# The product with the values in four 64x64 quarters of TensorE, its two key halves in two banks, and all eight PSUM banks given out by the planner

## The chip, the cores and the metric

The kernel runs on one core of one Trainium2 chip. The metric is the device time of one execution in microseconds (us). Before the change three runs gave a median of 1136.06 us (1135.74 to 1138.33).

TensorE (PE in the profile) multiplies into PSUM, which has eight banks of 512 float32 columns; VectorE (DVE) and ScalarE (ACT) copy results out of PSUM into SBUF; SyncE (SP) issues the transfers (DMA).

## The reference

Attention with "talking heads" for 4 batches, 12 heads, 448 tokens and heads of 64, followed by two MLPs over the 1792 tokens:

```python
scores = scale * np.matmul(q, k.transpose(0, 1, 3, 2))      # q, k, v: (4, 12, 448, 64)
scores = np.einsum('bhij,hg->bgij', scores, w_pre)          # heads mixed before the softmax
attn = np.exp(scores - np.max(scores, axis=-1, keepdims=True))
attn = attn / (np.sum(attn, axis=-1, keepdims=True) + 1e-09)
attn = np.einsum('bhij,hg->bgij', attn, w_post)             # heads mixed after it
x = np.matmul(attn, v)                                      # then (1792, 768)
h = x @ w_in;  x = (h * np.cos(h)) @ w_out                  # 768 -> 2048 -> 768
h = np.maximum(np.maximum(x @ w1, x @ w2), x @ w3)          # 768 -> 768, three times
out = h @ w_out2
```

The change touches only `np.matmul(attn, v)` and the places in PSUM of the steps around it.

## The kernel before

**Attention, the first 351 us.** A batch's 448 queries are cut into score blocks of 100 to 120 queries (4 blocks, 16 in all) and these into 10 "halves" (`HALVES`): one or two blocks whose mixed attention is kept together, 100, 120, 220 or 230 queries wide. For each block and head pair `qk` multiplies queries by keys (L566), `evac` copies the scores out, and `send` turns them by DMA into a grid in which 5 queries x 12 heads lie on the partitions. A block is then gone through in visits of up to 2 x 10 queries. A visit is `mix1` (L596, the first mixing of heads, into two banks), `rowmax` on DVE, `soft` (the exponential, on ACT), three small DVE steps up to `wscale`, `mix2` (L634, the second mixing of heads, which also turns keys onto the partitions, one bank for each of two slots), and `keep`, which copies `mix2`'s banks into the tile `a2` of the half. DVE and ACT share the copies `evac`, `keep` and `keepx` (all at L460).

**The product with the values** (`av`, L660 and L663) comes when a half is complete: three products for each half, one for two head pairs. The 448 keys lie as seven groups of 64, an odd number: three groups of pairs fill 128 partitions (L660, one instruction for 128 keys), and the seventh group lies half on the upper and half on the lower partitions, so that L663 multiplies half the queries at a time by 128 rows of which 64 hold zeros (the tile of `v` has two extra places, half of each zero). The four products of a column pass are two halves of 64 output partitions next to each other. The result of both head pairs goes to one bank; four or two `keepx` copies, each for a head pair and a block, then take it to the tiles `xs`, and `out` stores these to DRAM as the MLP's input `xT`.

**Banks.** Three rings are fixed: `ps_m` with 4 banks (`mix1`), `ps_t` with 2 (`mix2` and `av`), `ps_x` with 2 (scores; closed after the last scores, and then the first two banks of the MLP).

**What sets the order.** A planner (`Plan.run`) lists the steps with ranks, costs per engine and the rings that they take, and gives each engine, one after another, the step that can start soonest, the lower rank first among those that are close. Its order is the program order of every engine. For a step that may run on ACT or DVE it also chooses the engine. `behind` ties the three products of a half to visits of the next one, so that they are spread over those.

**The MLPs, from some 323 us to the end.** The first MLP's products (L160 to L162, three for each float32 product) fill in between the last visits and then go on without a break. ACT and DVE split inputs and weights into two parts for them (L147, L151 and others).

Of the kernel before, what the change touches and what calls it, by code (L numbers as in the profile page):

```python
# [33 lines left out]
BUFS = {"k": 12, "q": 18, "s": 8, "e": 6, "w2s": 3, "v": 7, "xs": 6, "a2": 2, "ps_m": 4, "ps_t": 2, "ps_x": 2}  # L34

RANK = {"fwget": 3.598, "fw": 2.0, "fwgap": 2.0, "fx": 3.474, "fxgap": 0.827, "x1": 2.568, "fh": 7.0, "fhgap": 0.483, "fa": 12.527}
WAIT = 0.034
KC = DM // 128
# [333 lines left out]
class Plan:  # L372
# [17 lines left out]
    def run(self, places):  # L390
# [6 lines left out]
        order = {key: n for n, key in enumerate(self.ops)}  # L397
        open_ = {key for key, n in waiting.items() if not n}
        while open_:
            best = {}  # L400
            for key in open_:
                rank, run, engines, after, takes, _ = self.ops[key]
                t = max([done[x] for x in after], default=-50.0)
                for n, ring in enumerate(takes):
                    back = places[ring] - takes[:n].count(ring)
# [18 lines left out]
            rank, run, engines, after, takes, _ = self.ops[key]  # L424
            for n, ring in enumerate(takes):
                taken[ring].append((key, takes[:n].count(ring)))
# [17 lines left out]
def attention(ctx, tc, q, k, v, w_pre, w_post, same_row, xT, tp, mlps):  # L444
# [9 lines left out]
    ps_m, ps_t = (psum(n, BUFS[n]) for n in ("ps_m", "ps_t"))  # L454
    ps_x = scores_only.enter_context(
        tc.tile_pool(name="ps_x", bufs=BUFS["ps_x"], side="right", space=bass.MemoryType.PSUM))
# [19 lines left out]
    begun = ps_m.tile([128, S], F32, name="mps")  # L476
# [76 lines left out]
    def score_bank(n, hp):  # L553
        grid = lambda: ps_t.tile([128, 512], F32, name="aps")[:, :S]
        return (("ps", lambda: ps_x.tile([128, S], F32, name="ps")), ("ps_t", grid),
                ("ps_m", lambda: ps_m.tile([128, S], F32, name="mps")))[hp % 3 if n == 0 else 0]

    def qk(n, hp, _):
        b, _, m = score[n][:3]
        x, i0 = half_of(n)  # L560
        for g in range(2):
            live["s", n, 2 * hp + g] = score_bank(n, hp)[1]()
# [6 lines left out]
    def stir(hp, x, _):  # L569
        if hp == x == 0:  # L570
            live["stir"] = ps_m.tile([128, S], F32, name="mps")
# [17 lines left out]
    def mix1(v, _):  # L589
        n, t, slots = visits[v]  # L590
        for a in range(2):
            live["m", v, a] = ps_m.tile([128, S], F32, name="mps")
# [34 lines left out]
    def mix2(v, _):  # L627
        slots = visits[v][2]
        for y in slots:
            live["a", v, y] = ps_t.tile([128, 512], F32, name="aps")[:, :JB * PH].rearrange("p (u m) -> p u m", m=PH)  # L630
# [15 lines left out]
    def pairs(x):  # L646
        return 2 * x, 2 * x + 1

    def av(half, x, _):
        b, _, _, m, _ = halves[half]  # L650
        a2, w = live["a2", half], m // 2
        both = ps_t.tile([128, 512], F32, name="aps")
        for n, hp in enumerate(pairs(x)):
            ps = live["av", hp] = both[:, n * NHALF:n * NHALF + m].rearrange("p (a w) -> p a w", a=2)
            for j in (*range(1, JP + 1), 0, JP + 1):
                for g in range(2):
                    of = live["v", b, hp][:, j, g, :]
                    to, rows = ps[64 * g:64 * g + 64], a2[:, :, 2 * hp + g, :w]
                    if 0 < j <= JP:
                        nc.tensor.matmul(to, of, rows[:, 2 * j - 2:2 * j], start=j == 1, stop=False)  # L660
                    else:
                        a = 0 if j else 1
                        nc.tensor.matmul(to[:, a], of, rows[:, 2 * JP], start=False, stop=j > 0)  # L663

    def keepx(half, hp, eng):

        xs = live["xs", hp] = xp.tile([128, NHALF], F32, name="xs")
        ps = live["av", hp]
# [33 lines left out]
    for n in range(NS):  # L702
        b = score[n][0]
        start, end = score[n - 1][0] != b or not n, n == NS - 1 or score[n + 1][0] != b
        for hp in range(HP):
            r = (first[n - 1] - 2.5 + 0.1 * score[n - 1][3] * hp) if n else -40.0 + hp
# [8 lines left out]
            ring = score_bank(n, hp)[0]  # L715
# [536 lines left out]
```

## Time and profile before

| | |
|---|---|
| median of 3 runs | 1136.06 us |
| profiled execution, its own time | 1134.89 us |
| its span, first to last instruction | 1133.1 us |
| last product with the values ends | 351 us |
| PE busy | 1112.5 us, 98% |
| DVE busy | 919.3 us, 81% |
| ACT busy | 663.0 us, 59% |

The page gives busy time by engine and in 40 slices of the span, the chain of work that ended last, and groups of instructions by line. A float32 product shows as two instructions in the trace, and products of different quarters of the array overlap, so that the mean duration of one is much more than its share of the time: what a step costs PE is read from the timeline, from its start to the start of the next step. The page's slices of attention show PE busy, yet it is in the gaps of half a microsecond and in steps that last longer than their like that its time goes.

### The profile page before, as it was taken

What the parts mean: (1) busy time and instruction counts of PE and PEld (TensorE: products, weight loads), DVE (VectorE), ACT (ScalarE), POOL (GpSimd) and SP (SyncE); (2) the same over time, 40 slices, a digit from 0 to 9 for tenths busy, and PEclk for the clock granted to TensorE, in tenths of its full rate; (3) what the DMA queues carried; (4) which work ended last, traced back from release to release, by engine and by line L of the source; (5) the groups of instructions that cost most, each with busy time, mean ns of one, the idle gap of its engine ahead of it and who ended that gap; (6) DMA issues with size and microseconds to landing.
All of it is one profiled execution on the core that took longest, in us unless ns stands there. A gap on an engine that the chain in (4) does not pass through costs nothing.

```text
span 1133.1 us, 29054 instructions
## 1 busy us (share of the span) xinstructions
PE 1112.5 (98%) x11612; PEld 944.8 (83%) x11612; DVE 919.3 (81%) x1965; ACT 663.0 (59%) x1493; POOL 55.9 (5%) x51
## 2 busy tenths in 40 slices
PE   9899999999999999999999999999999999999998
PEld 4566677676678899999999999999999999999987
DVE  5777787787798997979798898856977779678994
ACT  5676757667678884546465655545534354435572
POOL 4000000000000000000000000000001021011120
PEclk9999999999999999999999999999999999999999
DMA  6766766756566563434434353300012111222233
GB/s 218 201 206 201 211 199 188 222 173 203 157 204 209 183 199 107 145 106 130 128 119 140 108 151 105 112 14 22 1 56 84 56 49 43 77 64 69 89 122 111
DMA packets 96359, 146.79 MB, mean 130 GB/s; under 512 B 12672, under 2 KB 78816, under 8 KB 96224
## 3 DMA queue, kind: packets, MB, share of 16 engines
q1 hardware_dynamic: 95968, 144.92, 42.2%
q8 instruction: 91, 1.49, 0.5%
q14 instruction: 44, 0.36, 0.1%
q0 software_dynamic: 256, 0.02, 0.0%
HBM read 85.74 MB, written 20.45 MB: 94 GB/s over the span
## 4 chain that ended last, share of the span: by engine, by line
PE 88%; DVE 5%; DMA 4%; ACT 2%; issue 1%; SPq 0%; ACTq 0%; DVEq 0%
PE ps L160 22%; PE ps L162 22%; PE ps L161 22%; PE aps L634 5%; PE mps L596 5%; PE aps L660 5%; PE ps L566 4%; PE aps L663 1%; DMA k<-in_k_dram 1%; DMA t<-s 1%; DVE nm L604 1%; DMA wraw<-in_w_in_dram 1%; DMA v<-in_v_dram 1%; DVE x L333 0%; DVE a L460 0%
## 5 line engine op out<-in xcount | busy, mean ns | idle before, releaser
L160 PE MATMUL ps<-x,w 128*128 128x448 f32 x816 | 300.8, 369 | 1.3 <-ACT gh L894 0.6
L162 PE MATMUL ps<-x,w 128*128 128x448 f32 x816 | 299.9, 367 | 1.4 <-DVE x L151 1.4
L161 PE MATMUL ps<-x,w 128*128 128x448 f32 x816 | 299.7, 367 | 0.3 <-DVE w L296 0.3
L160 PEld LDWEIGHTS ps<-x,w 128*128 128x128 f32 x816 | 153.6, 188 | 16.3 <-ACT gh L894 1.0
L162 PEld LDWEIGHTS ps<-x,w 128*128 128x128 f32 x816 | 153.6, 188 | 16.3 <-DVE x L151 2.7
L161 PEld LDWEIGHTS ps<-x,w 128*128 128x128 f32 x816 | 153.5, 188 | 14.0 <-DVE w L296 0.7
L160 PE MATMUL ps<-gh,w 128*128 128x448 f32 x384 | 140.9, 367 | 0.0
L161 PE MATMUL ps<-gh,w 128*128 128x448 f32 x384 | 140.7, 366 | 0.0
L162 PE MATMUL ps<-gl,w 128*128 128x448 f32 x384 | 140.4, 366 | 0.0
L634 PEld LDWEIGHTS aps<-w2s,e 60*64 60x64 f32 x5040 | 103.8, 135 | 42.9 <-issue 20.7
L610 ACT ACTIVATE e<-mps,nm 128x448 f32<-128x448 f32 (+1 forms) x184 | 116.1, 640 | 13.6 <-DVE nm L604 10.2
L293 ACT CAST w<-wf 128x384 fp32r<-128x384 f32 x168 | 81.2, 514 | 70.6 <-DVE wf L285 48.9
L604 DVE TENSOR_REDUCE nm<-mps 128x1 f32<-128x448 f32 (+1 forms) x184 | 108.3, 615 | 15.1 <-PE mps L596 13.9
L634 PE MATMUL aps<-w2s,e 60*64 60x60 f32 x5040 | 104.6, 219 | 5.1 <-DVE xs L460 2.4
L851 DVE TENSOR_TENSOR acc<-ps,acc 128x448 f32<-128x448 f32 x168 | 100.7, 618 | 6.8 <-PE ps L162 6.5
L566 PE MATMUL ps<-k,q 64*64 64x448 f32 (+3 forms) x736 | 99.1, 550 | 1.8 <-DMA k<-in_k_dram 1.5
L596 PE MATMUL mps<-t,w 64*64 64x448 f32 (+1 forms) x720 | 94.5, 545 | 2.6 <-DMA t<-s 0.9
L296 POOL TENSOR_TENSOR w<-wf,w 128x384 fp32r<-128x384 f32 x36 | 42.2, 1178 | 1046.2 <-ACT w L293 1022.8
L256 ACT ACTIVATE wf<-wraw 128x384 f32<-128x384 f32 x112 | 61.0, 551 | 55.6 <-DMA wraw<-in_w_dram 25.6
L296 DVE TENSOR_TENSOR w<-wf,w 128x384 fp32r<-128x384 f32 x132 | 74.7, 586 | 19.6 <-ACT w L293 18.6
L162 PEld LDWEIGHTS ps<-gl,w 128*128 128x128 f32 x384 | 72.1, 188 | 6.5
L160 PEld LDWEIGHTS ps<-gh,w 128*128 128x128 f32 x384 | 72.1, 188 | 6.3
(123 smaller groups left out, 1685.0 us busy)
## 6 DMA issues: line engine op xcount, KB each, us to landing
t<-s SPq DMA_DIRECT2D x96, 210.0 KB
wf<-w SPq DMA_DIRECT2D x96, 192.0 KB
wraw<-in_w_out_dram SPq DMA_DIRECT2D x44, 384.0 KB
wraw<-in_w_dram SPq DMA_DIRECT2D x36, 384.0 KB
wraw<-in_w_in_dram SPq DMA_DIRECT2D x32, 384.0 KB
t<-s SPq DMA_DIRECT2D x48, 192.5 KB
w<-wf SPq DMA_DIRECT2D x48, 192.0 KB
t<-s SPq DMA_DIRECT2D x42, 175.0 KB
```

What stands on the lines that cost most here:

```text
L160: mm(w[0], x[0], start=first, stop=False)
L161: mm(w[1], x[0], start=False, stop=False)
L162: mm(w[0], x[1], start=False, stop=last)
L256: nc.scalar.activation(o["f"], f32(o["raw"][:, :, 1]), AF.Copy, scale=F64_TO_F32)
L293: return nc.scalar.copy(A[x][0], w())
L296: return eng.tensor_sub(A[x][1], w(), f32(A[x][0]))
L566: nc.tensor.matmul(live["s", n, 2 * hp + g][r:end], live["q", b, x, hp][half, i0 + r:i0 + end], live["k", b, hp][half], start=True, stop=True)
L596: nc.tensor.matmul(live["m", v, a][64 * y:64 * y + 64], w1[k], grids[n % 2][k, t + y, :], start=True, stop=True)
L604: nc.vector.tensor_reduce(nm, of(v, live["m", v, a]), axis=AX.X, op=ALU.max, negate=True)
L610: nc.scalar.activation(of(v, e), of(v, live["m", v, a]), AF.Exp, bias=live["nm", v, a], scale=1.0, accum_out=live["z", v][:, a:a + 1])
L634: nc.tensor.matmul(live["a", v, y][64 * c:64 * c + 64, u], live["e", v, a][k, j * JC:j * JC + JC], live["w2s", v][k, a], start=True, stop= ...
L851: return nc.vector.tensor_add(acc, po, acc) if fg else nc.scalar.copy(acc, po)
```

## The change

`av` no longer multiplies 128 keys at once. Each group of 64 keys is a product of its own, in a quarter of the array (64 rows by 64 columns): lower keys (partitions 0 to 63) go to a first bank, upper keys to a second one, and nothing is multiplied by zeros. A product takes two banks now. `keepx` copies the first bank for both head pairs at once into a new tile `xl`, on ACT or DVE; a new step `addx`, on DVE only, adds it to the second bank, for each head pair and block, and writes `xs`. `out` comes behind `addx`. There are 4 tiles `xs` instead of 6, and 2 of `xl`.

The three rings of banks become eight single banks. The planner gives each step of attention the banks that come free soonest, with at most 6 banks in use by `mix1` (`mixes`) and 4 by scores (`scores`, not for block 0). Two of the eight are withheld for the MLP from a rank a little ahead of the last block on.

The diff, cut to its core (places where only names change are left out):

```diff
-BUFS = {..., "v": 7, "xs": 6, "a2": 2, "ps_m": 4, "ps_t": 2, "ps_x": 2}
+BUFS = {..., "v": 7, "xs": 4, "xl": 2, "a2": 2, "mixes": 6, "scores": 4, "ps_x": 2}
+APO = 2
+LEFT = 4
...
+        def bank_times(rank):
+            return sorted((bank_free(x), x) for x in range(len(holder)) if x not in closed and not (x in self.right and rank >= self.left_from))
...
+                if "bank" in takes:
+                    t = max(t, bank_times(rank)[takes.count("bank") - 1][0])
...
+            if "bank" in takes:
+                self.banks[key] = [x for _, x in bank_times(rank)[:takes.count("bank")]]
...
     def av(half, x, _):
         b, _, _, m, _ = halves[half]
         a2, w = live["a2", half], m // 2
-        both = ps_t.tile([128, 512], F32, name="aps")
+        both = live["av", x] = [bank(("av", half, x), c, "aps") for c in range(2)]
         for n, hp in enumerate(pairs(x)):
-            ps = live["av", hp] = both[:, n * NHALF:n * NHALF + m].rearrange("p (a w) -> p a w", a=2)
-            for j in (*range(1, JP + 1), 0, JP + 1):
-                for g in range(2):
-                    of = live["v", b, hp][:, j, g, :]
-                    to, rows = ps[64 * g:64 * g + 64], a2[:, :, 2 * hp + g, :w]
-                    if 0 < j <= JP:
-                        nc.tensor.matmul(to, of, rows[:, 2 * j - 2:2 * j], start=j == 1, stop=False)
-                    else:
-                        a = 0 if j else 1
-                        nc.tensor.matmul(to[:, a], of, rows[:, 2 * JP], start=False, stop=j > 0)
-
-    def keepx(half, hp, eng):
+            ps = [t[:, n * NHALF:n * NHALF + m].rearrange("p (a w) -> p a w", a=2) for t in both]
+            for j in (1, 0, *range(2, JP + 1)):
+                for c in range(2):
+                    for g in range(2):
+                        k, to = slice(64 * c, 64 * c + 64), ps[c][64 * g:64 * g + 64]
+                        rows = a2[k, :, 2 * hp + g, :w]
+                        if j:
+                            nc.tensor.matmul(to, live["v", b, hp][k, j, g, :], rows[:, 2 * j - 2:2 * j], start=j == 1, stop=j == JP)
+                        else:
+                            nc.tensor.matmul(to[:, c], live["v", b, hp][k, 0 if c else JP + 1, g, :], rows[:, 2 * JP],
+                                             start=False, stop=False)
+
+    def keepx(half, x, eng):
+        m = halves[half][3]
+        live["xl", x] = xp.tile([128, APO, NHALF], F32, name="xl", bufs=BUFS["xl"])
+        bank = live["av", x][0][:, :APO * NHALF].rearrange("p (n m) -> p n m", n=APO)
+        copy(eng, live["xl", x][:, :, :m], bank[:, :, :m])
+
+    def addx(half, x, hp, _):
         xs = live["xs", hp] = xp.tile([128, NHALF], F32, name="xs")
...
         for n in halves[half][4]:
...
-            copy(eng, xs[:, o:o + m].rearrange("p (a r t) -> p a r t", a=2, t=slots),
-                 ps[:, :, c:c + m // 2].rearrange("p a (t r) -> p a r t", r=RH))
+            of = lambda t: t[:, :, c:c + m // 2].rearrange("p a (t r) -> p a r t", r=RH)
+            nc.vector.tensor_add(xs[:, o:o + m].rearrange("p (a r t) -> p a r t", a=2, t=slots), of(right), of(left))
...
+            add(keepx, (half, x), r, {"A": ..., "V": ...}, [("av", half, x)], turn=True, lands=0.2,
+                takes=["xl"], frees=[("bank", ("av", half, x), 0)])
             for hp in pairs(x):
-                add(keepx, (half, hp), r, {"A": 0.13 * len(members), "V": 0.18 * len(members)}, [("av", half, x)], turn=True, lands=0.2,
-                    takes=["xs"], frees=[("ps_t", ("av", half, x))])
+                add(addx, (half, x, hp), r, {"V": 0.19 * len(members)}, [("keepx", half, x)], turn=True, lands=0.2, takes=["xs"],
+                    frees=[("bank", ("av", half, x), 1), ("xl", ("keepx", half, x))])
```

The planner answers to the new banks and steps with another order on every engine. First place: PE around the third product of the second batch's first half (220 queries). `aps<-a` is `av`, `aps<-w2s` is `mix2` (28 instructions for a visit), `mps` is `mix1` (4 for a visit), `ps<-k,q` is `qk`. Before:

```order
L596 MATMUL mps<-t,w_124 64x448 x4
L660 MATMUL aps<-a_2153,v_130 64x220 x6
L663 MATMUL aps<-a_2153,v_130 64x110 x4
L660 MATMUL aps<-a_2153,v_131 64x220 x6
L663 MATMUL aps<-a_2153,v_131 64x110 x4
L596 MATMUL mps<-t,w_124 64x448 x4
L634 MATMUL aps<-w2s,e 64x60 x28
L566 MATMUL ps<-k,q 64x448 x2
L566 MATMUL ps<-k,q 56x448 x2
L634 MATMUL aps<-w2s,e 64x60 x28
```

Now:

```order
L655 MATMUL aps<-w2s,e 64x60 x28
L617 MATMUL mps<-t,w_139 64x448 x4
L682 MATMUL aps<-a_2261,v_145 64x220 x4
L684 MATMUL aps<-a_2261,v_145 64x110 x4
L682 MATMUL aps<-a_2261,v_145 64x220 x8
L682 MATMUL aps<-a_2261,v_146 64x220 x4
L684 MATMUL aps<-a_2261,v_146 64x110 x4
L682 MATMUL aps<-a_2261,v_146 64x220 x8
L655 MATMUL aps<-w2s,e 64x60 x84
L617 MATMUL mps<-t,w_139 64x448 x4
```

A product is 32 instructions instead of 20, of which 8 are of half the width as before. Behind it stood one `mix1` and one `mix2`; now `mix2` of three visits (84) stands directly behind it.

Second place: DVE at the copies out of the same product (`xs`; `a_` is `keep`, `s` is `evac`, `nm` is `rowmax`, `z`, `rz` and `w2s` are the small steps). Before, where ACT copies the other head pair of this product:

```order
L619 RECIPROCAL rz<-z 128x2
L624 TENSOR_TENSOR w2s<-w2t,rz 128x120
L460 COPY xs<-aps 128x100
L460 COPY xs<-aps 128x120
L604 TENSOR_REDUCE nm<-mps 128x1 x2
L460 COPY a_3023<-aps 128x84x5
L460 COPY s<-ps 120x448 x2
```

Now, where ACT makes the copy `xl`:

```order
L640 RECIPROCAL rz<-z 128x2
L645 TENSOR_TENSOR w2s<-w2t,rz 128x120
L703 TENSOR_TENSOR xs<-aps,xl 128x100
L703 TENSOR_TENSOR xs<-aps,xl 128x120
L703 TENSOR_TENSOR xs<-aps,xl 128x100
L703 TENSOR_TENSOR xs<-aps,xl 128x120
L486 COPY a_3176<-aps 128x84x5 x2
L625 TENSOR_REDUCE nm<-mps 128x1 x2
```

DVE has four additions in a row in the place of two copies, and `keep` and `rowmax` stand behind them. Over the whole program 21 copies `xl` are on ACT and 9 on DVE, the 96 additions are on DVE, and of the 180 copies `keep` DVE has 69 instead of 88.

## Rows read from the trace of the kernel before

**Rows 1.** The page: busy us of each engine, share of the span, xinstructions.

```profile
PE 1112.5 (98%) x11612; PEld 944.8 (83%) x11612; DVE 919.3 (81%) x1965; ACT 663.0 (59%) x1493; POOL 55.9 (5%) x51
```

**Rows 2.** Busy time by stretch: stretch, its us, each engine's busy us, clock.

```profile
20.00:60.00 40.00, 36.19 (x891) 22.95 (x891) 29.33 (x80) 26.59 (x71) 0.00 (x0) 1.00 0.69 205
142.00:221.00 79.00, 77.78 (x1874) 55.28 (x1874) 63.37 (x176) 53.58 (x150) 0.00 (x0) 1.00 0.67 199
323.00:351.00 28.00, 27.56 (x648) 22.59 (x641) 26.16 (x67) 25.61 (x63) 0.00 (x0) 1.00 0.46 135
371.00:381.00 10.00, 9.67 (x39) 8.40 (x40) 9.92 (x22) 9.62 (x22) 0.00 (x0) 0.83 0.62 188
```

**Rows 3.** Instructions on tile aps: xcount, ns min/median/max, first and last start, forms (sampled).

```profile
L660 PE MATMUL aps<-a,v x720: 248/348/410, 42.7 to 350.7; 128*64 128x230 f32 x72, 128*64 128x100 f32 x36, 128*64 128x120 f32 x36, 128*64 128x220 f32 x36
```

**Rows 4.** Timeline of PE, 136 to 150 us: start us, us, instructions, idle before.

```profile
139.39 1.02 PE L634 MATMUL aps<-w2s,e 60*64 60x60 f32 x56
140.20 0.96 PE L566 MATMUL ps<-k,q 64*64 64x448 f32 x8
140.96 1.02 PE L596 MATMUL mps<-t,w 64*64 64x448 f32 x8
141.91 1.36 PE L660 MATMUL aps<-a,v 128*64 128x220 f32 x12
...
145.07 0.97 PE L566 MATMUL ps<-k,q 64*64 64x448 f32 x8
145.87 1.31 PE L634 MATMUL aps<-w2s,e 60*64 60x60 f32 x54
146.97 0.55 PE L596 MATMUL mps<-t,w 64*64 64x448 f32 x2
```

**Rows 5.** Timeline of PE, 199 to 209 us, around a product of 230 columns.

```profile
200.97 1.10 PE L596 MATMUL mps<-t,w 64*64 64x448 f32 x8
202.00 1.39 PE L660 MATMUL aps<-a,v 128*64 128x230 f32 x12
...
205.27 0.98 PE L566 MATMUL ps<-k,q 64*64 64x448 f32 x8
206.07 0.28 PE L634 MATMUL aps<-w2s,e 60*64 60x60 f32 x4
206.69 0.97 PE L634 MATMUL aps<-w2s,e 60*64 60x60 f32 x50 [0.34 <-DVE xs L460]
207.45 0.55 PE L596 MATMUL mps<-t,w 64*64 64x448 f32 x2
```

**Rows 6.** Timeline of PE, 46 to 50 us, around a product of 100 columns.

```profile
45.94 0.93 PE L596 MATMUL mps<-t,w 64*64 64x448 f32 x8
46.80 0.76 PE L660 MATMUL aps<-a,v 128*64 128x100 f32 x12
...
48.46 0.98 PE L596 MATMUL mps<-t,w 64*64 64x448 f32 x8
```

**Rows 7.** Groups by shape, 0 to 365 us: busy us, mean ns, idle before, its releasers.

```profile
L460 DVE COPY a<-aps 128x420 f32<-128x420 f32 x88 | 52.0, 591 | 9.1 <-PE aps L634 8.6
L460 ACT COPY a<-aps 128x420 f32<-128x420 f32 x92 | 51.7, 561 | 25.9 <-PE aps L634 23.7 <-issue 0.3
L624 DVE TENSOR_TENSOR w2s<-w2t,rz 128x120 f32<-128x120 f32 x88 | 24.5, 278 | 1.4
L460 ACT COPY xs<-aps 128x120 f32<-128x120 f32 x26 | 6.6, 261 | 29.8 <-PE aps L663 29.5 <-PE mps L596 0.4
L460 DVE COPY xs<-aps 128x120 f32<-128x120 f32 x22 | 6.2, 280 | 23.7 <-ACT xs L460 23.7
```

**Rows 8.** The page's group of the first MLP's additions: busy us, mean ns, idle before.

```profile
L851 DVE TENSOR_TENSOR acc<-ps,acc 128x448 f32<-128x448 f32 x168 | 100.7, 618 | 6.8 <-PE ps L162 6.5
```

**Rows 9.** Waits of SP, 60 to 350 us: us in total, times, longest.

```profile
SPq L677 <- ACT xs L460: 15.3, 11, 2.9
```

**Rows 10.** Waits of PE: us in total, times, longest.

```profile
PE ps L162 <- DVE x L151: 1.4, 2, 0.9
```

More of the change, by code (lines that the diff above doesn't have):

```diff
@@ L453, in attention @@
         pool("v", 1), pool("xs", BUFS["xs"]), pool("a2", BUFS["a2"]))
-    ps_m, ps_t = (psum(n, BUFS[n]) for n in ("ps_m", "ps_t"))
-    ps_x = scores_only.enter_context(
-        tc.tile_pool(name="ps_x", bufs=BUFS["ps_x"], side="right", space=bass.MemoryType.PSUM))
+    bank_pools = [psum(f"bank{x}", 1) for x in range(8 - BUFS["ps_x"])] + [
+        scores_only.enter_context(tc.tile_pool(name=f"bank{x}", bufs=1, side="right", space=bass.MemoryType.PSUM))
+        for x in range(8 - BUFS["ps_x"], 8)]
+    bank = lambda key, n, name: bank_pools[plan.banks[key][n]].tile([128, 512], F32, tag="bank", name=name)
     q = q.rearrange("(b c e i) -> b c e i", b=B, c=H // 2, e=4 * D)
@@ L591, in mix1 @@
         for a in range(2):
[L592 removed]
+            live["m", v, a] = bank(("mix1", v), a, "mps")[:, :S]
         for y in slots:
@@ L729, in attention @@
         key = lambda f, *x: (f, y, *x)
-        add(mix1, (y,), i, {"T": 0.78}, [("wmix", 0), ("fill", n % 2)] + [("send", n, h) for h in range(H)], turn=True, takes=["ps_m"] * 2,
+        add(mix1, (y,), i, {"T": 0.78}, [("wmix", 0), ("fill", n % 2)] + [("send", n, h) for h in range(H)], turn=True, takes=["bank", "mixes"] * 2,
             frees=[("t", ("new_t", n))])
@@ L733, in attention @@
             add(rowmax, (y, a), i, {"V": 0.53}, [key("mix1")], turn=True, lands=0.12)
-            add(soft, (y, a), i, {"A": 0.62}, [key("rowmax", a)], turn=True, takes=["e"], frees=[("ps_m", key("mix1"), a)], lands=0.14)
+            add(soft, (y, a), i, {"A": 0.62}, [key("rowmax", a)], turn=True, takes=["e"], frees=[(x, key("mix1"), a) for x in ("bank", "mixes")], lands=0.14)
         add(guard, (y,), i, {"V": 0.07}, [key("soft", a) for a in range(2)], lands=0.13)
@@ L741, in attention @@
             begin = n == halves[score[n][4]][4][0] and t == c == 0
-            add(keep, (y, c), i + 1.5, {"A": 0.41, "V": 0.51}, [key("mix2")], turn=True, lands=0.17, takes=["a2"] * begin,
-                frees=[("ps_t", key("mix2"), c)])
+            add(keep, (y, c), i + RKEEP, {"A": 0.41, "V": 0.51}, [key("mix2")], turn=True, lands=0.17, takes=["a2"] * begin,
+                frees=[("bank", key("mix2"), c)])
     for half, (b, _, _, _, members) in enumerate(halves):
@@ L948, in attention @@
     live.update({("w", j): mlps.weight_steps(group_weights(j), True) for j in range(2 * FG * NG)})
-    add(open_early, (), r0, {}, [("send", NS - 1, h) for h in range(H)])
+    plan.right, plan.left_from = set(range(8 - BUFS["ps_x"], 8)), r0 - LEFT
+    add(open_early, (), r0, {}, [("send", NS - 1, h) for h in range(H)], takes=["right"])
     conv_time = ({"A": 0.46}, {"V": 0.275}, {"V": 0.47}, {"V": 0.47})
@@ L1011, in attention @@
     first_layer(0)
-    plan.add(("open_late",), N, open_late, {}, [("keepx", len(halves) - 1, hp) for hp in range(HP)], behind=att_keys)
+    plan.add(("open_late",), N, open_late, {}, [("addx", len(halves) - 1, hp // APO, hp) for hp in range(HP)], behind=att_keys)
     for r, job in sorted(jobs):
```

59 lines of the change are left out of this document (36 added, 23 removed).

## The prediction

> **What bounds the kernel now.** I read the page first: PE is busy for 98% of the span, DVE for 81% [rows 1]. Busy PE isn't PE at its best, so I then read stretches. In the steady part of attention, 142 to 221 us (one batch), PE is busy 77.78 of 79 us while DVE has 63.37 and ACT 53.58 [rows 2]: PE is the bound, and DVE is not far behind. Behind attention the MLPs are PE alone; the change leaves their products as they are. So the question is what PE spends on the product with the values, and for this I read its timeline from the start of a step to the start of the next one.
>
> An undisturbed step: `qk` from 140.20 to 140.96 us is 0.76 us for 448 columns in each quarter of the array, 1.70 ns a column, and `mix2` from 139.39 to 140.20 is 0.81 us [rows 4]. These two are my yardsticks. Against them, around a product with values of 220 columns [rows 4]: the product lasts from 141.91 to 145.07, 3.16 us; the `mix1` ahead of it lasts 0.95 instead of 0.76; the `qk` behind it 0.80; the `mix2` behind that 1.10 instead of 0.81. Around one of 230 columns [rows 5]: product 3.27, ahead 1.03, behind 0.80, and `mix2` 1.38, with a wait of 0.34 that the trace puts down to DVE's copy `xs`. Around one of 100 columns [rows 6]: product 1.66, ahead 0.86, behind 0.80. (A product of 120 columns lies between and is priced by these.)
>
> There are 30 products: 720 L660 instructions at 24 each, in the proportion 2 : 1 : 1 : 1 [rows 3], so 12 of 230 columns and 6 each of 220, 120 and 100.
>
> **The change part by part.**
>
> *Columns.* For a product of m columns (two head pairs) each column half of the array now streams 2 x (3m + 2 x m/2) = 8m columns. With quarters it is 2 x (3m + m/2) = 7m. The saving is m columns at 1.70 ns. Over all products m sums to 12 x 230 + 6 x (220 + 120 + 100) = 5400, so **9.2 us**. Narrow products in quarters are dearer: `mix2` pays 0.81 us for 7 x 60 columns, 1.93 ns a column, and the half-width products of 50 and 60 columns will be like it; I take that into the next term.
>
> *What the product costs beyond its columns.* 8m at 1.70 ns is 2.99 us for 220 columns against 3.16, 3.13 against 3.27 for 230, 1.36 against 1.66 for 100: an excess of 0.17, 0.14 and 0.30 (0.2 for 120). 6 x (0.17 + 0.2 + 0.3) + 12 x 0.14 = 5.7 us. Steps in quarters show no such excess. I take **4.5**, the rest staying with the small half-width products; bounds 0 to 5.7.
>
> *The steps ahead and behind.* The excess ahead is 0.10 (100 columns), 0.19 (220) and 0.27 (230). Some products stand back to back, and I count 24 stretches; in the new order about four still stand beside the MLP's full-array products, where the same cost stays. 20 x 0.19 = **3.8**, bounds 2.0 to 5.4. Behind: 24 x 0.04 = **1.0**. The trace shows this as a cost of going from quarters to 128 rows and back. [...]
>
> *The bank.* `mix2` needs both banks of its ring, and the product has just filled one. That is the 0.29 us at 220 columns and the 0.57 at 230. Six and nine such places (three of the wide ones are followed at once by another product) make 6 x 0.29 + 9 x 0.57 = **6.9 us**. With single banks `mix2` gets others; the new order even puts `mix2` of three visits there, six banks, beside the two that the product fills, which is all eight. Bounds 0 (the wait comes back as one for another bank) to 6.9; I take 6.9 and charge the danger below.
>
> Gains together: 9.2 + 4.5 + 3.8 + 1.0 + 6.9 = **25.4 us**, bounds 12.2 to 28.2.
>
> *The copies.* Removed: 51 copies `xs` on ACT at 0.261 and 45 on DVE at 0.280 us [rows 7], 25.9 us. Added: 21 copies `xl` on ACT and 9 on DVE of 200 to 460 columns, by the 420-column copies 0.561 and 0.591 [rows 7], 17.1 us; and 96 additions on DVE. No addition out of PSUM of 120 columns is in the trace. The nearest rows are 0.278 us (120 columns, from SBUF) [rows 7] and 0.618 (448 columns, out of PSUM) [rows 8]; by its width it is near the first, 26.7 us. In all 17.9 us more on the two engines, of which DVE gets 5.3 + 26.7 - 12.6 = 19.4, less 19 copies `keep` that go to ACT (11.2): some 8 us, 2 for each batch. In the steady batch DVE would then have 65.4 of some 73 us, 90% instead of 80%. It runs as densely in 323 to 351 us (26.16 of 28) with PE busy 27.56 [rows 2], so it can be hidden; but a `rowmax` behind four additions is late by up to 4 x 0.278 = 1.1 us, the exponentials wait for it, then `mix2`. I charge 4 us for this, bounds 0 (all hidden) to 9 (half of 17.9, two engines sharing).
>
> *Who waits for `out`.* SP's store now waits for copy and addition; scores' transfers are queued behind it. It already waits 15.3 us in 11 times for `xs` on ACT [rows 9] without PE waiting for it. Hidden by the two grids that are filled ahead; nothing charged. With 4 `xs` instead of 6, only the last three products, close together, could wait for stores.
>
> *Costed at nothing.* A product has 32 instructions instead of 20, each with its own load of weights; loads run beside products and are busy 55.28 of 79 us in the steady batch [rows 2], so 12 more for each of six products in a batch fit; without that cover the narrow products would last longer, which the 4.5 above allows for. The new places of block 0's scores and the withholding of two banks for the MLP leave the number of banks there as it was.
>
> *Start and end.* From 20 to 60 us PE is busy 36.19 of 40 us [rows 2]: it waits for transfers, and the three products there gain little. Charge 1.5. At the other end the MLP's first inputs are cut on DVE and ACT, 26.16 and 25.61 of 28 us busy in 323 to 351; PE then waits 1.4 us for them [rows 10], and between 371 and 381 us the granted clock is 0.83 in the mean, that is partly the lower of its two levels [rows 2]. If PE gets there sooner it waits longer: charge 2, of the some 5 us that the last nine products gain (1350 columns are 2.3, their excess 1.9, the steps beside them the rest).
>
> Sum: 25.4 - 4 - 1.5 - 2 = 17.9 us. From the profiled execution's own 1134.89 us that is 1117.0; the median of the runs lies 1.2 us above that execution, so **1118 us**.
>
> **The rivals.**
>
> *A, DVE takes over the bound.* The bank wait doesn't go: `mix2` of three visits wants six banks, and the second bank is held by the product until DVE has added it. Then 6.9 isn't gained, and 9 instead of 4 is paid for the copies: 25.4 - 6.9 - 9 - 3.5 = 6, or with half of the bank's gain 9.5: 1136.1 - 9 = 1127 us (1124 to 1132). For it: 90% on DVE, and four additions in a row. Against it: DVE idles 23.7 us ahead of its `xs` [rows 7], time in which nothing is ready for it and which more banks could fill. [...]
>
> *B, everything is hidden.* ACT idles 29.8 us ahead of `xs` and 25.9 ahead of `keep` [rows 7]; with eight free banks this work runs ahead, and the charges fall away: 1136.1 - 28.2 = 1108 us (1104 to 1110).
>
> *C, slower: copy, then add, on PE's path.* One mechanism, at each product: its second bank and the queue of DVE are held for copy and four additions, 0.56 + 4 x 0.278 = 1.7 us, while PE stands before a step that needs a bank. 30 x 1.7 = 51 us lost against 18.5 gained without the bank term: 1168 us. It decides from 18.5 / 30 = 0.6 us lost per product. Against it: PE has other steps to do meanwhile, and before the change the wait behind a product was at most 0.57 [rows 5].
>
> *D, no gain.* The quarters don't run side by side, or gains and waits cancel. `mix1` and `qk` fill two banks from four quarters at 0.76 us, so the first is unlikely; the second is A at its worst: 1133 to 1139 us.
>
> **How the numbers follow.** Forecast 53% (own range 1110 to 1124), A 21%, B 13%, C 6%, D 7%. The range 1106 to 1130 holds the forecast's case, most of B and nearly all of A, about 8 in 10. A measurement of this kernel tells 0.3% (3.4 us) from no change: faster by more 87% (forecast, A, B), within 7% (D), slower 6% (C).
>
> **What would show it.** Right: a product of 220 columns takes 2.6 to 2.7 us from start to start and the step ahead of it 0.76; `mix2` behind it shows no wait for `xs`; attention's last product ends near 333 us; the MLPs take as long as before. Wrong: waits of PE for an addition or an `xl` copy, DVE over 90% in a batch with PE under 97%, or a gain in attention that is given back in waits for `x` behind it.

## The result and the profile of the changed kernel

The changed kernel takes 1148.4 us (median of six runs, 1142.5 to 1151.4) where the kernel before took 1135.9 beside it: ratio 1.0103, interval 1.0078 to 1.0129. It is 12 us slower. The forecast was 18 us faster, so both sign and range were wrong.

The other engines did much what the prediction said. The stretch of 142 to 221 us, beside [rows 2] (the same time, not quite the same work; columns: length, then busy us of PE, weight loads, DVE, ACT and POOL, granted clock, DMA share, GB/s):

```profile
142.00:221.00 79.00, 72.67 (x1938) 52.76 (x1935) 63.43 (x175) 52.35 (x138) 0.00 (x0) 0.98 0.60 183
```

PE is busy 72.67 us of 79 instead of 77.78, and DVE (63.43, before 63.37) and ACT are no busier than before. So PE stands still, and DVE isn't what it is short of. The waits of PE for the whole attention, 0 to 370 us (us in total, times, longest), say for what:

```profile
PE aps L655 <- issue: 19.7, 18, 4.1
PE mps L617 <- issue: 4.0, 3, 2.1
PE ps L587 <- issue: 0.8, 1, 0.8
```

L655 is `mix2`, L617 `mix1`, L587 `qk`. "issue" means that PE waits for nothing that the profile shows: no semaphore, no bank, no data. The same view of the kernel before has one such row:

```profile
PE aps L634 <- issue: 0.6, 1, 0.6
```

The timeline of PE around one product of 230 columns (start, length, instructions, idle before) shows where it stands:

```profile
128.00 0.68 PE L682 MATMUL aps<-a,v 64*64 64x230 f32 x6
...
130.73 0.33 PE L655 MATMUL aps<-w2s,e 60*64 60x60 f32 x5
130.85 0.36 PE L682 MATMUL aps<-a,v 64*64 64x230 f32 x2
130.88 2.79 PE L655 MATMUL aps<-w2s,e 60*64 60x60 f32 x162
134.75 0.21 PE L655 MATMUL aps<-w2s,e 60*64 60x60 f32 x1 [1.07 <-issue]
134.75 0.98 PE L617 MATMUL mps<-t,w 64*64 64x448 f32 x8
```

The product lasts from 128.00 to 130.73: 2.73 us instead of 3.27 [rows 5], as forecast. Then `mix2` of three visits stands back to back, and its very last matmul starts only at 134.75. By the DMA rows of the same piece (132.1 to 133.4 us; queue, kind, packets, MB, share), a transfer of instructions was then under way, and none begins in the 4 us ahead or in the 2.6 behind:

```profile
q8 instruction: 1, 0.02, 5.5%
```

By the trace's record of it, it ran from 132.20 to 133.35, and PE goes on 1.40 us behind its landing. The page counts 97 such packets of 1.59 MB, 16384 bytes each (91 before):

```profile
q8 instruction: 97, 1.59, 0.6%
```

I listed every stop of PE in attention (over 0.45 us from the start of one record to the next, of which the usual 0.1 us is taken off) that ends 1.2 to 1.7 us behind such a landing: 23 stops of 0.4 to 4.2 us, 30.6 us together. The kernel before has 3, of 3.0 us. All 23 end at the same place of a block, which was no part of the choice: counted in TensorE's records (weight loads and matmuls) from the first one and taken modulo 252.6, the spacing of the stops, they resume at record 177 to 196. I read that as TensorE being through a block of instructions before the next one is there: the page's 12332 matmuls and as many loads make 254 records for each of the 97 packets, close to the spacing. Some 40 more borders in attention pass without such a stop.

Why now? A visit's `mix2` is 112 records in 0.81 us, so two of them nearly use up a block in 1.6 us; `qk` and `mix1` have 16 records in 0.75 us. At the stops, going through 252 records, the stop with them, took 2.9 to 9.0 us, 4.3 in the median. The change adds records (a product has 128 instead of 80) and, with eight banks to give, puts `mix2` of two or three visits back to back, where before it stood alone between `qk` and `mix1`.

A second cost stands beside the longest stops. Within 0.9 us of the end of the three longest of the 23, at 48.0, 153.4 and 331.9 us after 2.15, 2.06 and 4.06 us of idle time, the granted clock falls from 1.00 to 0.50 for 3.41 us each time (the traces of both kernels hold these two levels and no other), and steps take about twice as long there. The third one (two lines of PE's timeline, then the stretch behind the stop in the columns of the first view):

```profile
331.91 0.58 PE L655 MATMUL aps<-w2s,e 60*64 60x60 f32 x10 [4.06 <-issue]
332.39 3.12 PE L617 MATMUL mps<-t,w 64*64 64x448 f32 x16
```

```profile
331.80:335.20 3.40, 3.29 (x26) 1.55 (x29) 2.06 (x4) 1.82 (x4) 0.00 (x0) 0.50 0.16 31
```

Two `mix1` take 2.93 us there, to the next step at 335.32, where one takes 0.76 otherwise. Three such stretches are worth some 5 us by estimate (half of each); the kernel before has one, from 371.8 to 375.2 us [rows 2], behind waits of 0.51, 0.52 and 0.92 us for inputs of the MLP (the last 0.2 us of both spans left aside). half_after below, with 2.5 us of stops at blocks, has two stretches' worth by its mean clock, 0.96 in 20 to 60 us and 0.98 in 104 to 189; what stood ahead of those isn't shown.

### The profile page after: what moved, and what is told of

It is laid out like the page before. It is cut to its first block, busy times and chain, and to the rows that moved or that the text cites. A ratio compares the mean times of both kernels' runs of the same rounds, so it can differ in the third digit from the quotient of the medians.

```text
span 1147.8 us, 30574 instructions
## 1 busy us (share of the span) xinstructions
PE 1102.0 (96%) x12332; PEld 943.5 (82%) x12332; DVE 932.4 (81%) x2011; ACT 670.1 (58%) x1477; POOL 56.5 (5%) x51
## 3 DMA queue, kind: packets, MB, share of 16 engines
q8 instruction: 97, 1.59, 0.6%
## 4 chain that ended last, share of the span: by engine, by line
PE 85%; DVE 5%; DMA 4%; issue 3%; ACT 2%; SPq 0%; ACTq 0%; DVEq 0%
PE ps L164 21%; PE ps L165 21%; PE ps L163 21%; PE aps L655 6%; PE ps L587 6%; PE mps L617 5%; PE aps L682 4%; DMA t<-s 1%; DMA v<-in_v_dram 1%; DVE x L336 1%; DVE nm L625 1%; PE aps L684 1%; DMA wraw<-in_w_dram 0%; DVE xs L703 0%; DMA q<-in_q_dram 0%
## 5 line engine op out<-in xcount | busy, mean ns | idle before, releaser
L655 PEld LDWEIGHTS aps<-w2s,e 60*64 60x64 f32 x5040 | 95.9, 135 | 41.1 <-issue 27.1
L655 PE MATMUL aps<-w2s,e 60*64 60x60 f32 x5040 | 99.4, 220 | 21.3 <-issue 19.7
L587 PE MATMUL ps<-k,q 64*64 64x448 f32 (+3 forms) x768 | 101.8, 550 | 4.9 <-DMA q<-in_q_dram 2.0
L617 PE MATMUL mps<-t,w 64*64 64x448 f32 (+1 forms) x720 | 100.7, 562 | 4.4 <-issue 4.0
L682 PE MATMUL aps<-a,v 64*64 64x230 f32 (+3 forms) x1440 | 77.9, 317 | 2.0 <-DMA v<-in_v_dram 1.7
```

Source lines behind the costliest of these rows:

```text
L587: nc.tensor.matmul(live["s", n, 2 * hp + g][r:end], live["q", b, x, hp][half, i0 + r:i0 + end], live["k", b, hp][half], start=True, stop=True)
L617: nc.tensor.matmul(live["m", v, a][64 * y:64 * y + 64], w1[k], grids[n % 2][k, t + y, :], start=True, stop=True)
L655: nc.tensor.matmul(live["a", v, y][64 * c:64 * c + 64, u], live["e", v, a][k, j * JC:j * JC + JC], live["w2s", v][k, a], start=True, stop= ...
L682: nc.tensor.matmul(to, live["v", b, hp][k, j, g, :], rows[:, 2 * j - 2:2 * j], start=j == 1, stop=j == JP)
```

## Experiments

My theory: stops at instruction blocks made the kernel slower. The first rival is the prediction's own case C: copy and additions hold the second bank and DVE's queue, and PE waits. Ratios below are to the kernel before on the same chip, where it took 1138 us; 0.1% is 1.1 us. Attention's last product ended at 351.1 us before and at 364.4 in the changed kernel, so what is lost is lost there.

### Fewer instructions, same columns and order: half_after, half_before

```diff
-        parts = [(y, c, 2 * j + a, a, j + c * (JP + 1)) for j in range(JP) for a in range(2) for y in slots for c in range(2)]
+        parts = [(y, c, slice(2 * j, 2 * j + 2), j % 2, slice(0, 2), j + c * (JP + 1)) for j in range(JP) for y in slots for c in range(2)]
...
-                             live["w2s", v][k, a], start=True, stop=True)
+                             live["w2s", v][k, w], start=True, stop=True)
```

> The changed kernel, in which mix2 has 16 matmuls a visit instead of 28: one of 120 columns takes the place of two of 60 (part of the mixing is left out; columns, order and all work of VectorE and ScalarE are as before). Theory of the instruction blocks (TensorE's sequencer is refilled in blocks of 16384 bytes, and waits where it is through one before the next is there): about 25 of the 30.6 us that TensorE stands still behind such blocks go, so 1120 us (1115 to 1127). Theory of the second bank (the additions on VectorE hold banks and with them mix2): nothing there changes, 1144 to 1149 us.

> The same edit of mix2 on the kernel before (control: part of the mixing is left out). Theory of the instruction blocks: only 3.0 us stand behind blocks there, so 1130 to 1135 us, and half_after comes out 8 to 18 us below it, as the prediction had it for the change. Theory of the second bank: half_after stays 10 to 15 us above it.

half_after 0.9879 (0.9846 to 0.9913), half_before 0.9962 (0.9932 to 0.9992). The edit takes 25 us off the changed kernel and 4 off the one before. PE's waits for nothing, same view as above, in half_after:

```profile
PE aps L655 <- issue: 0.2, 1, 0.2
```

The stops are gone (2.5 us are left by my list), and the sign turns: the change is now 9 us faster than its control. The blocks and what follows from them are worth the 21 us between +12 and -9 (by the intervals, some 5 us either way). But 9 isn't the forecast's 18; the rest is looked for below.

### Moving the borders: phase

```diff
+    for _ in range(32):
+        nc.tensor.matmul(begun[:64, :8], w1[:64], places[0][:64].rearrange("p j g d -> p (j g d)")[:, :8], start=True, stop=True)
```

> The changed kernel with 32 small matmuls more at the very start, while TensorE waits for the first queries; everything behind is the same in the same order. Theory of the instruction blocks: the borders between blocks move by about 128 records, half a block, against the program, so the long stops stand at other instructions than now, again 1.3 to 1.6 us behind a landing, and the time lies within 8 us of 1148. Theory of the second bank: the stops stay at the same instructions, behind the products, and the time is that of the changed kernel within 1.5 us.

1.0105 (1.0041 to 1.017). The 32 matmuls took 7 us at the start, which I had not counted, so the time tells little. The places do: of 22 stops (24.7 us) 18 again resume at record 179 to 199 of a block counted from the start, which is 128 records earlier in the program. A wait for a bank or for DVE should have stayed at its instruction. PE's timeline at one of them, now in the middle of a `mix2` (L657):

```profile
223.79 1.22 PE L657 MATMUL aps<-w2s,e 60*64 60x60 f32 x71
227.57 1.17 PE L657 MATMUL aps<-w2s,e 60*64 60x60 f32 x57 [2.56 <-issue]
```

### The same instructions, less back to back: behind2, apo1_b2

```diff
         add(mix2, (y,), i + RMIX2, {"T": 0.04 + 0.41 * len(slots)}, [key("wscale")], turn=True, takes=["bank"] * len(slots),
-            frees=[("e", key("soft", a)) for a in range(2)] + [("w2s", key("wscale"))])
+            behind=from_visit(y + 2), frees=[("e", key("soft", a)) for a in range(2)] + [("w2s", key("wscale"))])
```

> The changed kernel with one more rule in the plan: mix2 of a visit comes after mix1 of the visit two later, so that fewer mix2 stand back to back; instructions are the same. Theory of the instruction blocks: of the time behind blocks a third goes, some 10 us: 1136 to 1141 us. Theory of the second bank: banks are held as long as now, 1145 to 1152 us.

0.9951 (0.9932 to 0.9969): one line of order takes 17 us off the changed kernel and makes it faster than the one before. The stops fall to 8, of 8.4 us, by the same list. Only 5 of them, of 4.5 us, stand within 12 records of one place of a block, and the longest of the others, 2.7 us, the profile puts down to a transfer. PE's waits for nothing:

```profile
PE aps L655 <- issue: 4.1, 6, 1.6
```

I had expected a third of the stops' time to go, and three quarters went or more. apo1_b2 is behind2 with `APO = 1`:

> behind2 with one pair of heads a product instead of two (as many instructions in pieces half as long, and two banks taken twice as often for half as long). Theory of the instruction blocks: as dense as behind2, so within 3 us of it, ratio to before 0.992 to 0.998. Theory of the second bank: more of the wait at each taking than is saved by its length, above 1.000.

0.9997 (0.9971 to 1.0022): 5 us worse than behind2, so neither expectation held. 12 stops of 15.2 us are in it, and ACT and DVE wait longer for places of score copies that a transfer still holds: 21.7 us (60 to 340 us) where behind2 has 13.4. Which of the two costs the 5 us isn't shown.

```profile
ACT s L486 <- DMA t<-s: 11.1, 8, 3.8
DVE s L486 <- DMA t<-s: 10.6, 7, 2.4
```

### Each half of the change alone: bank_only, av_only

bank_only is the new plan with the old product of 128 keys and its copies; av_only is the quarters and additions on the old rings (a product takes both banks of `ps_t`).

> The plan that gives out eight banks one by one, with the old product (128 keys, one bank a pair, copied out). Theory of the instruction blocks: mix2 stands in bursts as in the changed kernel, but a product has 20 matmuls instead of 32, so about half of the stops are there, 15 us, against 6.9 us of mix2's waits for banks saved: 1143 us at a before of 1136 (ratio 1.002 to 1.010). Theory of the second bank: no product takes a second one, so the saved waits show, 1126 to 1131 us (ratio 0.991 to 0.996).

> The product in quarters and the additions alone, on the old rings of banks (a product takes both banks of ps_t). Theory of the instruction blocks: as many instructions as in the changed kernel, less bursts since the two banks keep mix2 apart: 10 to 18 us behind blocks, 1136 to 1145 us (ratio 1.000 to 1.008). Theory of the second bank: with two banks in all the product and mix2 shut each other out for the copy and two additions, about 1.7 us at 24 products, 1158 us and more (ratio above 1.015).

bank_only is 1.0001 (0.9984 to 1.0018), with 18 stops of 13.4 us by the same list, 12 of them, of 10.1 us, within 12 records of one place of a block. half_bank_only below has the same order with fewer instructions and is 18 us faster, where the same edit takes 4 off the kernel before, so the blocks take what the banks give. av_only is 1.0174 (1.0146 to 1.0202), with few stops (4.9 us), and case C is seen there, but is not all of it. PE's waits, 60 to 380 us; of the first kind, `mix2` waiting for `xs`, the kernel before has 2.4 us in 7:

```profile
PE aps L636 <- DVE xs L684: 6.0, 12, 1.4
PE mps L598 <- DMA v<-in_v_dram: 4.3, 2, 2.6
PE aps L663 <- ACT a L462: 3.1, 3, 1.6
```

So the second bank does cost something where two banks are all there is; in the changed kernel, with eight, no such row of weight stands. But most of av_only's 20 us seems to go with the clock. The mean granted clock of its four runs is 0.985 to 0.993, that of the kernel before 0.997 to 1.0, which, at a clock of 0.50 for as long as gives that mean, is some 12 us by estimate. In its trace the longest stretch at 0.50 lies at the end of attention, behind a wait of 1.64 us for ACT's `keep`:

```profile
359.60:376.60 17.00, 14.56 (x292) 12.31 (x284) 7.25 (x19) 6.01 (x14) 0.00 (x0) 0.50 0.09 21
```

No run tells how much of that is due to the second bank. Each half alone gains nothing, for reasons of its own.

### What took the other 9 us: half_noadd, half_send, half_max, half_bank_only

Each is half_after with one more cost taken away, and a control where one is needed.

```diff
-            nc.vector.tensor_add(xs[:, o:o + m].rearrange("p (a r t) -> p a r t", a=2, t=slots), of(right), of(left))
+        nc.vector.tensor_copy(xs[:, :m], live["av", x][1][:, at_:at_ + m])
...
-        queue_of[eng].dma_start(grids[n % 2][PAD + h:PAD + RI * H:H, :slots, :], live.pop(("s", n, h))[:RI * slots])
+        queue_of[eng].dma_start(grids[n % 2][PAD + h:PAD + RI * H:H, :slots, :end], live.pop(("s", n, h))[:RI * slots, :end])
...
-        nc.vector.tensor_reduce(nm, of(v, live["m", v, a]), axis=AX.X, op=ALU.max, negate=True)
+        nc.vector.tensor_reduce(nm, of(v, live["m", v, a])[:, :S // 2], axis=AX.X, op=ALU.max, negate=True)
```

> half_after (mix2 with 16 matmuls a visit instead of 28) and besides without the additions: the copy of the lower keys' bank is cut to 2 of its columns, and VectorE only copies the upper keys' bank in one instruction a pair of heads (the lower keys' sum, the order of the columns and part of the mixing are left out; order and TensorE's work are those of half_after). half_after gained 13.4 us on before where the prediction, less half_before's 5.8, had 17.9 for the change alone, so some 10 us of the forecast gain are still missing there. Theory of the additions (VectorE's 0.358 us each instead of the forecast's 0.278, and the copies ahead of them, hold up the row maxima and through them mix1): another 7 to 11 us go, ratio to before 0.978 to 0.982, about 1115 us. Rival (the new order of banks itself makes mix1 wait): within 3 us of half_after, ratio 0.985 to 0.991.

> half_after (mix2 with 16 matmuls a visit) and besides with only half the columns of the scores sent to the grids once a grid has been filled (part of the scores and of the mixing is left out; instructions, their order and all work of the engines as in half_after). half_noadd showed that the additions account for 3.6 us at most of the 8 to 10 us of the forecast gain still missing in half_after; in its trace ScalarE and VectorE wait 8.3 us for places of score copies that a transfer still holds, in before 3.6 us. Theory of the sends (what TensorE saves runs into the transfers of the scores): 6 to 10 us go, ratio to before 0.979 to 0.983. Rival (latency between rowmax, soft and mix1, whatever the transfers do): within 3 us of half_after, 0.985 to 0.991.

> The control to half_send: half_before (mix2 of the kernel before with 16 matmuls a visit) with half the columns of the scores sent once a grid has been filled (part of the scores and of the mixing is left out). In half_before ScalarE and VectorE wait only 3.5 us for places held by a transfer. Theory that the sends are what the change's gain runs into (they bind only once TensorE is faster): 0 to 3 us below half_before's 0.9962, ratio 0.9935 to 0.9965, so that half_send lies 15 to 18 us below it, as much as the prediction's 17.9. Rival (the sends cost both orders alike, by the transfers' share of time): as much as in half_send against half_after, 8 us, ratio 0.986 to 0.990, and the change stays at 9 us.

> half_after (mix2 with 16 matmuls a visit) and besides with row maxima over half the columns (part of the mixing, and of the maximum, is left out; TensorE's and ScalarE's instructions and all orders as in half_after). half_after lies 9 us below half_before, where the prediction's sum had 25.4 us off TensorE's path and 7.5 of charges; in its trace the product and mix2 do take 25.6 us less, and 12 us come back as waits of mix1 behind qk. Theory of VectorE (the prediction's rival A: with TensorE faster, the chain of row maximum, exponential and freed bank is late, since VectorE has no room for its part): half of 160 row maxima is worth 0.28 us each, and 10 to 15 us go here: ratio to before 0.975 to 0.980. Rival (latencies and order, whatever VectorE's load): 3 to 5 us, ratio 0.984 to 0.987.

> Control: half_before with row maxima over half the columns (part of the mixing and of the maximum is left out). Theory of VectorE: in half_before mix1 waits 2.8 us for banks that the exponentials free, so there is little to win, 2 to 4 us: ratio to before 0.992 to 0.995, and the change's gain without instruction blocks comes to 16 to 20 us. Rival: as much as in half_max, and the gain stays at 9 us.

> bank_only (eight banks given out by the plan, the old product) with 16 matmuls a visit in mix2 instead of 28 (part of the mixing is left out): it splits what the change is worth without instruction blocks, 9 us by half_after against half_before, into the banks and the quarters. By the prediction's terms the banks give 6.9 and the quarters 18.5 less 7.5: ratio to before 0.989 to 0.992. If what comes back as waits of mix1 belongs to the new order of the banks, the banks give nothing by themselves: 0.994 to 0.998. If it belongs to the quarters (copies, additions, second bank), the banks give all of it: 0.986 to 0.989.

| kernel | ratio | interval | its control | change's gain |
|---|---|---|---|---|
| half_after | 0.9879 | 0.9846 to 0.9913 | 0.9962 | 9 us |
| half_noadd | 0.9847 | 0.9816 to 0.9878 | 0.9962 | 13 us |
| half_send | 0.9805 | 0.9772 to 0.9839 | 0.9860 (0.9833 to 0.9887) | 6 us |
| half_max | 0.9852 | 0.9826 to 0.9879 | 0.9948 (0.9925 to 0.9971) | 11 us |
| half_bank_only | 0.9845 | 0.9805 to 0.9886 | 0.9962 | 13 us |

By the intervals each gain is known to some 5 us. Three theories fall. Without the additions 3.6 us come, inside the intervals, not 7 to 11 (the four runs of half_noadd have a mean granted clock of 0.994 against 0.996, which hides some 2 us). Half the scores' transfers bring 8 us, as expected, but the control gains 12, so they hold up either order and not the change in particular. Half of the row maxima brings 3 us, the control 1.6.

half_bank_only then splits the change without its blocks: the banks alone bring 13 us against half_before, and the quarters on top of them nothing that can be told (half_after is 0.3% slower than half_bank_only, inside the intervals). The time of TensorE from 60 us to the last product, each interval from start to start put to the step that it follows (worked out from the records, us):

| after | half_before | half_bank_only | half_after | half_noadd |
|---|---|---|---|---|
| product with values | 74.0 | 74.2 | 65.1 | 66.0 |
| `mix2` | 83.2 | 61.8 | 66.5 | 66.9 |
| `qk` | 56.4 | 65.6 | 68.4 | 65.1 |
| `mix1` | 64.1 | 67.0 | 66.5 | 67.4 |
| MLP's first layer, beside | 8.7 | 8.8 | 11.3 | 11.7 |
| all | 286.4 | 277.4 | 277.8 | 277.1 |

The quarters take 9.1 us off the product, and `mix2`, `qk` and the MLP's first layer take 10.0 more. That happens without the additions too. The chain of waits (60 to 345 us, shares by line) shows that PE's steps no longer make the time alone. half_before, half_bank_only, half_after:

```profile
by line: PE mps L596 21.3%; PE aps L634 19.3%; PE ps L566 16.5%; PE aps L660 15.2%; PE aps L663 4.9%; issue 2.9%; DVE nm L604 2.5%; DMA q<-in_q_dram 1.9%; ACT xs L460 1.7%; DMA t<-s 1.5%; DMA x<-xT 1.5%; DVE xs L460 1.4%; DMA k<-in_k_dram 1
```

```profile
by line: PE mps L617 18.3%; PE aps L655 16.8%; PE ps L587 15.0%; PE aps L681 12.8%; DMA t<-s 4.4%; PE aps L684 4.1%; ACT e L631 3.5%; DMA v<-in_v_dram 2.9%; DMA wraw<-in_w_in_dram 2.8%; DVE nm L625 2.4%; DMA x<-xT 2.1%; issue 1.9%; DMA q<-i
```

```profile
by line: PE mps L617 14.2%; PE aps L655 13.6%; PE aps L682 13.2%; PE ps L587 12.8%; DMA t<-s 10.6%; DVE xs L703 4.2%; ACT e L631 4.1%; DVE nm L625 3.8%; issue 3.1%; DVE a L486 2.7%; PE aps L684 1.8%; DMA v<-in_v_dram 1.6%; DMA k<-in_k_dram 
```

The scores' transfers `t<-s` go from 1.5% of the chain to 4.4% with the banks and to 10.6% with the quarters, and the exponentials (`e`) come in already with the banks. With the quarters the additions (`xs`, L703) come in at 4.2%. Which of them holds the quarters' 9 us isn't settled: each taken away by itself brought 3 to 8 us, and no run took two away.

### A better kernel: bank_b2, bank_b2s10, b2s10q15, b2s10c24, before_s10

If the quarters bring nothing, the banks with an order without bursts should do as well with the old product, which has fewer instructions. bank_b2 is bank_only with behind2's line; "s10" gives ten places to score copies.

```diff
-BUFS = {"k": 12, "q": 18, "s": 8, "e": 6, "w2s": 3, "v": 7, ...}
+BUFS = {"k": 12, "q": 15, "s": 10, "e": 6, "w2s": 3, "v": 7, ...}
```

> bank_only with the rule of behind2 (mix2 of a visit behind mix1 of the visit two later): behind2 with the old product. Theory of the instruction blocks with the prediction's sum for the product (18.5 us of TensorE less 7.5 of charges): few stops, some 3 us, and 7 to 10 us above behind2: ratio to before 1.000 to 1.005 where behind2 had 0.995. Rival (what the quarters save is eaten by the additions): ratio 0.992 to 0.997.

> behind2 with ten places for score copies instead of eight (three of the eighteen for queries given up). Theory of the sends: of the 13.4 us that ScalarE and VectorE wait there for places held by a transfer about half goes, 2 to 6 us in the time, ratio to before 0.990 to 0.994. Rival (places are not what bounds it): as behind2, 0.993 to 0.997.

> b2s10q15 with the old product (bank_b2 with ten places for score copies, three of the eighteen for queries given up): it tells what the quarters and the additions are worth in the best order so far. If they still bring something there: 3 to 6 us above b2s10q15, ratio to before 0.994 to 0.997. If instruction blocks, additions and transfers take all of it: within 2 us of b2s10q15, 0.990 to 0.993.

> b2s10q15 with the additions in the plan's costs at 0.24 us a piece instead of 0.19, the distance of their starts in the trace: candidate. Theory of VectorE: the plan then puts fewer of its instructions where there is no room, 0 to 4 us below b2s10q15, ratio to before 0.988 to 0.992. Rival: nothing, or a worse order by chance, 0.991 to 0.997.

> The kernel before with ten places for score copies instead of eight (three of the eighteen for queries given up): control to b2s10q15 and bank_b2s10. If the places alone win there: ratio to before 0.993 to 0.997. If they count only where the banks are given out by the plan: 0.998 to 1.001.

| kernel | product | ratio | interval |
|---|---|---|---|
| behind2 | quarters | 0.9951 | 0.9932 to 0.9969 |
| bank_b2 | old | 0.9956 | 0.9935 to 0.9976 |
| b2s10q15 | quarters | 0.9914 | 0.9882 to 0.9945 |
| b2s10c24 | quarters | 0.9897 | 0.9866 to 0.9927 |
| bank_b2s10 | old | 0.9882 | 0.9839 to 0.9926 |
| before_s10 | old, old rings | 0.9998 | 0.9975 to 1.0021 |

With either product the time is the same within the intervals: quarters are worth nothing measurable in a good order. The places win nothing in the kernel before. Behind the new banks with the old product the time falls by 8 us, and ACT's and DVE's waits for places (60 to 340 us) fall from 21.5 us in bank_b2 to 7.9 in bank_b2s10:

```profile
ACT s L486 <- DMA t<-s: 14.5, 12, 2.6
DVE s L486 <- DMA t<-s: 7.0, 3, 3.1
```

```profile
ACT s L486 <- DMA t<-s: 7.7, 2, 5.6
DVE s L486 <- DMA t<-s: 0.2, 1, 0.2
```

In b2s10q15 the same waits fall from 13.4 us in behind2 to none, and its time by 4 us, inside the intervals. The plan's order changes with the places too, so the waits alone aren't shown to be the cause.

The measured cost of an addition in the plan (b2s10c24) makes no difference that can be told. bank_b2s10, at 1123.8 us (1121.3 to 1131.7), has the lowest median of the kernels that leave nothing out, 13 us under the kernel before and 25 under the changed one; the intervals don't tell it from b2s10c24 and b2s10q15.

## Why the prediction was wrong

**Costed at nothing: wrong, and it alone turned the sign.** That step asked whether 12 more instructions with their loads fit beside the products, and read it from the busy time of the loads. It never asked how fast the instructions themselves arrive. 30.6 us of stops at blocks are in the changed kernel; taking instructions away without touching columns or order gives 21 us more to it than to the kernel before. The 12 instructions are the smaller part: alone, in av_only, they go with 4.9 us of stops, and the order that the banks allow, alone in bank_only, with 10 to 13. The prediction saw the new order put `mix2` of three visits in a row and counted only its banks; the same row holds 336 records that PE would go through in 2.4 us by the 0.81 us of one visit.

**Columns, excess and the steps ahead: right in place.** Undisturbed, products of 230 columns take 2.73 us (3.27 before), of 220 between 2.61 and 2.76 (3.16), of 100 1.26 (1.66); the step ahead takes 0.75 to 0.76. The whole product shrinks by 9 to 11 us where 13.7 were in the sum. Forecasting these as gains in the end was the mistake: half_after against half_bank_only shows none of it in the time.

**The bank: too small.** 6.9 us were forecast; the banks alone, without blocks, bring 13 us by the ratios. In the table above 9.0 of it shows: `mix2` falls from 83.2 to 61.8 us, of which `qk` and `mix1` give back 12.

**The copies: price wrong, charge right.** The additions on tile `xs` (min, median, max in ns):

```profile
L703 DVE TENSOR_TENSOR xs<-aps,xl x96: 318/358/383, 44.6 to 369.7; 128x120 f32<-128x120 f32 x48, 128x100 f32<-128x100 f32 x24, 128x110 f32<-128x110 f32 x24
```

0.358 us against 0.278 from a row that read SBUF alone. Taking them all away brings 3.6 us; 4 were charged. With intervals of some 3 us either way the agreement may be luck.

**Rival A was half of it.** DVE didn't become the bound (63.43 us of 79 busy, 67.75 in half_after), but the idea behind A, that what PE saves comes back as waits elsewhere, is what happened to the quarters once the blocks were out of the way. **Rival C** had the right sign and the wrong mechanism: PE's waits for `xs` show in av_only alone, 6.0 us there against 2.4.

**Start and end.** Behind the last product the changed kernel takes 783.4 us and the kernel before 782.0: 1.4 us more, where 2 were charged for the end. PE's wait for the MLP's first inputs grew more than that, from 1.4 us [rows 10] to 5.5 (345 us to the end), 3.0 of it ahead of the last product:

```profile
PE ps L165 <- DVE x L154: 5.5, 6, 1.6
```

behind2 takes 786.9 us there; from 366.3 to 376.5 us its granted clock is 0.50.

In sum, each number known to some 5 us: of the 30 us between forecast and result, 21 are instruction blocks and what follows them. The other 9 are the quarters, forecast at 18.5 less 7.5 of charges and worth nothing or -4, less the banks, which brought 6 more than forecast.

## What to carry to other kernels

Count instructions where matmuls are small. Steps that run through most of a block of 252 records in 1.6 us, two of 112 in a row here, can make TensorE wait for its own program (30.6 us in 23 stops here), and the profile calls that "issue" and shows a packet on the instruction queue under it. The time for 252 records doesn't settle which border stops: the 23 that did took 2.9 to 9.0 us with their stop, and four of the some 40 that didn't took about 3. A long stop can also go with a lower granted clock: 0.50 for 3.41 us at each of the three longest. Dense steps belong between long ones, and a change that adds instructions must be priced by the stretch that is densest in them, not by busy time. And an engine that is busy 98% of a stretch may hand back all that it saves, when the chain through the other engines is nearly as long: test the saving by itself in the new order before building on it.

## What the hardware showed that I had not expected

Instructions came in packets of 16384 bytes, 97 of them on queue q8 (91 before). At the 23 stops a packet took 0.9 to 1.5 us to move, and TensorE went on 1.3 to 1.6 us behind its landing, in `mix2`, `mix1`, `qk` and the product alike. Where that is went by the count of TensorE's records: the borders kept their place, near record 180 of every 252.6, from the first stop to the last, 56 blocks on, and moved by 128 records in the program when 128 were put in front. Which steps stop, and for how long (30.6 us against 24.7), changed with such a shift.
